# Pooled attention and a gated MLP on one core: first batch's left-over rows on ScalarE's queue, and a new order of work

## The chip, the core and the metric

The kernel runs on one core of a Trainium2 chip. The time is that of one execution on the device, in microseconds (us). Engines are named as in the profile: PE is TensorE, PEld its weight load, DVE is VectorE, ACT is ScalarE, POOL is GpSimd, SP is SyncE, which issues nearly all DMAs.

## The reference

Inputs: q, k, v of 8 batches x 8 heads x 576 rows x 64; weights w_in (512 x 1024), w_out (512 x 512) and w_sg (576 x 576), of which w_in and w_out arrive in 64-bit floats.

```
k_p = k.reshape(B, H, 72, 8, D).mean(axis=3);  v_p likewise
attn = softmax(q @ k_p.T / sqrt(D))                # 576 x 72 a head
x = (attn @ v_p), heads side by side               # 576 x 512 a batch
h = gelu(x @ w_in);  u, v = halves of h
v_n = (v - mean(v)) / sqrt(var(v) + 1e-6) * g_ln
gated = u * (w_sg @ v_n + b_sg)
out = x + gated @ w_out
```

## The kernel before

Batches go through the engines one after the other, each overlapped with its neighbours. A head pair is the unit of attention (four a batch, numbered 0 to 3). The work is cut into small generators, one for each letter, and a token such as `S0+1` advances step S for pair 0 of batch 1 by one piece. The table PROLOGUE (L23) lists all tokens of the program in the order in which they are issued; PERIOD is empty. Every engine works through its own instructions in that order and waits where an operand isn't there.

The letters, with what each does on the engines:
- A, B load half of k or v of a batch (tile kvraw, 512 KB), C a pair's q (tile qnat for batch 0, with pieces of 256 bytes; qraw later), E the left-over pooled rows of k and v that don't fill a tile (tile left, 256 KB in three DMAs). All of these, and the weights (lv, lu, lo, ls), go through `load`, with SP's queue by default.
- K pools k into kp and writes the scaled keys kbd (for batch 1 PE pools: `pool8`). K2 adds the left-over keys (lp). P pools v into vb.
- Q turns q into qT. S multiplies qT by kbd, takes the negated maximum (nmax, L559), the exponentials (e, L578, ten instructions on ACT) and the norm (L589, L590, L224).
- T and L turn the attention weights; V makes x from them; H and U make the two halves of gelu(x @ w_in); W the product with w_sg; O the product with w_out; Z and X store.
- v, u, o, s prepare the weights: each 64-bit weight is cut into a high and a low float (L286 to L294 and POOL's L231, L238).

Matmuls with the big weights run as three products of high and low parts. Rotating tiles: two `mps` and two `aps` PSUM tiles; a step that takes one waits until what used that tile two turns ago is read.

DMAs issued from SP and ACT carry one of eight completion semaphores in turn (DMAHW0 to DMAHW7); a DMA that comes round to a semaphore still in use waits for the earlier transfer to land, and what is behind it on that queue waits too.

The set OTHER (L87) names instructions that go to the second of two engines (for example `k01`: pooling of batch 0's second key half on DVE, otherwise POOL).

Of the kernel before, what the change touches and what calls it, by code (L numbers as in the profile page):

```python
# [28 lines left out]
u0 s2 S1+1 S1+1 s2 lu1 s2 H2+0 u1 C2+1 S0+1 Q2+1 S1+1 lo1 H2+0 S0+1 H0+0 o0 S1+1 P1+1 B0+1 u2 S2+1 o1 S0+1 H0+0 H2+0
H0+0 U0+0 S2+1 u3 V2+0 P1+1 S2+1 u2 u3 u2 U0+0 S1+1 H2+0 P0+1 S2+1 V1+0 u3 V3+0 P0+1 H0+0 H2+0 Q3+1 U1+0 P2+1 o2 H4+0  # L30
U1+0 H4+0 P2+1 S3+1 T0+1 S3+1 S3+1 H1+0 H2+0 H1+0 H0+0 S2+1 H4+0 H3+0 u3 A0+2 o2 H4+0 u2 P2+1 S3+1 H0+0 U2+0 S3+1 H3+0
L0+1 U3+0 A1+2 o2 H1+0 T0+1 P2+1 o2 H3+0 E0+2 T0+1 K2+2 C1+2 L0+1 Q1+2 L0+1 V0+1 V0+1 T1+1 T2+1 U2+0 H4+0 C0+2 H1+0
U3+0 K0+2 T1+1 T1+1 V1+1 Q0+2 K1+2 T2+1 T2+1 C3+2 T3+1 V1+1 H1+0 H3+0 B0+2 H3+0 H1+0 H3+0 B1+2 V2+1 H4+0 K2+2 H4+0
T3+1 H4+0 T3+1 P1+2 W2+0 V1+1 V3+1 V2+1 K2+2 P0+2 W2+0 C2+2 W1+0 V3+1 o3 K2+2 o3 V2+1 A0+3 S1+2 S1+2 S0+2 W0+0 W1+0 o3
S1+2 V0+1 o3 W1+0 S0+2 Q3+2 Q2+2 W0+0 S0+2 W3+0 W0+0 V0+1 W2+0 W3+0 V3+1 S1+2 S0+2 P2+2 S1+2 W1+0 H1+1 W2+0 V3+1 P2+2
C0+3 H3+1 H3+1 S3+2 H1+1 W0+0 A1+3 W3+0 S2+2 W3+0 S3+2 O0+0 H3+1 T0+2 H1+1 C1+3 K1+3 O0+0 O0+0 S0+2 S3+2 T0+2 T1+2
P2+2 O2+0 O2+0 U3+1 Z0+0 S2+2 H1+1 O2+0 P2+2 S2+2 H3+1 Z2+0 B1+3 H0+1 S3+2 U3+1 S3+2 H3+1 O1+0 H3+1 S2+2 Z0+0 H0+1
Z2+0 S2+2 L0+2 K0+3 V2+1 H1+1 O1+0 T2+2 V1+1 H4+1 L0+2 O1+0 H0+1 H4+1 H4+1 H0+1 T0+2 L0+2 H1+1 T0+2 H4+1 U0+1 L0+2
E0+3 H2+1 Z1+0 H0+1 V0+2 Q0+3 U0+1 O3+0 K2+3 H0+1 O3+0 L0+2 H2+1 H2+1 H4+1 Z1+0 B0+3 O3+0 P1+3 T1+2 U1+1 H2+1 K2+3
H2+1 T1+2 U2+1 H2+1 H4+1 T3+2 K2+3 T1+2 P0+3 Z3+0 A1+4 U1+1 H4+1 V0+2 H4+1 V1+2 K2+3 T2+2 W2+1 U2+1 S0+3 V1+2 W1+1  # L40
T2+2 W2+1 S0+3 T2+2 V1+2 W1+1 Q1+3 V2+2 K1+4 C2+3 W0+1 W2+1 T3+2 S0+3 Q2+3 C3+3 V2+2 T3+2 W1+1 W2+1 S0+3 T3+2 W3+1
T0+3 V3+2 Z3+0 S1+3 V0+2 W0+1 V3+2 W3+1 S1+3 S2+3 P2+3 W1+1 C0+4 V3+2 S2+3 T0+3 W0+1 V2+2 S1+3 S1+3 U2+2 H2+2 U2+2
S0+3 Q3+3 P2+3 P2+3 S3+3 C1+4 H2+2 W0+1 H2+2 O0+1 W3+1 W3+1 V1+2 O0+1 V3+2 A0+4 O1+1 P2+3 S3+3 S2+3 O0+1 V2+2 S2+3
# [903 lines left out]
```

## Time and profile before

| | |
|---|---|
| median of 3 runs (range) | 564.82 us (564.66 to 565.15) |
| the profiled execution | 566.29 us |
| its span, first to last instruction | 564.6 us |
| PE busy | 537.1 us, 95% |
| DVE, ACT, POOL busy | 421.1, 326.3, 287.2 us |
| DMA | 68.18 MB, mean 121 GB/s |

The profiled execution took 1.69 us more than its span and 1.47 us more than the median. All stretches below are in microseconds from the start of the span. A row of the timeline gives start, duration, engine, line, operation, tiles, and in brackets the idle time of that engine just before and what ended it.

### The profile page before, as it was taken

Reading aid. Unit: us, or ns where it says so; the run is one execution under the profiler, and the core shown is the slowest. Engines: PE = TensorE matmul, PEld = TensorE weight load, DVE = VectorE, ACT = ScalarE, POOL = GpSimd, SP = SyncE. Lnnn points to the kernel's source line nnn. Section 1 sums busy time; section 2 is a strip of 40 time slices with the busy share of each in tenths; the row PEclk is TensorE's granted clock in tenths of the full one; section 3 lists DMA queues with packets and bytes.
Section 4 is the critical chain, followed back from the end, with each engine's and each line's share of the span. In section 5 each row is a group of like instructions: output and inputs, shape, how many; then the busy total and the mean of one; then the engine's idle time right before and its main releaser. Section 6 shows DMA issues by size and latency. Waiting matters only on the chain.

```text
span 564.6 us, 10659 instructions
## 1 busy us (share of the span) xinstructions
PE 537.1 (95%) x3645; PEld 506.1 (90%) x3645; DVE 421.1 (75%) x655; ACT 326.3 (58%) x1057; POOL 287.2 (51%) x370
## 2 busy tenths in 40 slices
PE   4498898999999999999999999999999999999997
...
GB/s 211 299 307 157 113 135 48 130 59 161 132 176 102 91 157 129 138 102 139 128 135 96 127 111 149 158 146 103 120 152 86 128 65 73 69 24 1 22 43 106
DMA packets 186726, 68.18 MB, mean 121 GB/s; under 512 B 150832, under 2 KB 171056, under 8 KB 186672
## 3 DMA queue, kind: packets, MB, share of 16 engines
...
## 4 chain that ended last, share of the span: by engine, by line
PE 68%; DVE 9%; ACT 7%; SPq 7%; DMA 5%; issue 2%; POOL 1%; DVEq 0%; ACTq 0%; POOLq 0%
PE mps L141 56%; PE aps L141 12%; SPq L241 7%; ACT e L578 2%; DMA raw<-in_moe_w_out 1%; DVE nmax L559 1%; DMA qnat<-in_q 1%; DMA out<-y 1%; DVE e L224 1%; ACT L208 1%; DVE vbl L509 1%; DVE bst L746 1%; DVE vg L752 1%; DMA tfar<-y 1%; DMA y<-kfar 1%
## 5 line engine op out<-in xcount | busy, mean ns | idle before, releaser
L141 PE MATMUL mps<-xhl,wih 128*128 128x288 f32 x512 | 89.7, 297 | 1.4 <-ACT vg L742 1.0
L578 ACT ACTIVATE e<-aps,nmax 128x72 f32<-128x72 f32 x280 | 85.2, 355 | 9.7 <-DVE nmax L559 9.7
L141 PE MATMUL mps<-wih,xhl 128*128 128x512 f32 x256 | 83.8, 393 | 1.3 <-DVE wsl L321 1.3
L141 PEld LDWEIGHTS mps<-xhl,wih 128*128 128x128 f32 x512 | 75.4, 189 | 3.1 <-ACT vg L742 1.4
L578 ACT ACTIVATION_READ_ACCUMULATOR e<-aps,nmax 128x1 f32 x280 | 67.3, 241 | 0.0
L238 POOL TENSOR_TENSOR glo<-u,ghi 128x576 fp32r<-128x576 f32 x24 | 37.0, 1550 | 48.1 <-DVE ghi L213 24.4
L141 PEld LDWEIGHTS mps<-wih,xhl 128*128 128x128 f32 x256 | 48.1, 188 | 11.5 <-issue 1.7
L396 POOL TENSOR_TENSOR kvraw<-kvraw 128x512 f32<-128x512 f32 (+1 forms) x46 | 50.1, 1089 | 13.8 <-DMA kvraw<-in_k 7.6
L749 POOL TENSOR_TENSOR rstd<-mv,eps 128x1 f32<-128x1 f32 (+1 forms) x40 | 13.0, 325 | 86.5 <-DVE mv L747 83.9
L141 PE MATMUL mps<-wsh,vhh 128*128 128x288 f32 x256 | 55.1, 296 | 0.1
L141 PE MATMUL mps<-wsh,vhl 128*128 128x288 f32 x256 | 54.8, 295 | 0.0
L141 PE MATMUL mps<-xhl,wil 128*128 128x288 f32 x256 | 54.7, 295 | 0.0
L141 PE MATMUL mps<-wsl,vhh 128*128 128x288 f32 x256 | 54.7, 294 | 0.0
L141 PE MATMUL mps<-ghi,woh 128*128 128x288 f32 (+1 forms) x232 | 51.8, 302 | 0.1
L141 PE MATMUL mps<-glo,woh 128*128 128x288 f32 (+1 forms) x232 | 50.8, 298 | 0.4 <-POOL glo L238 0.4
L141 PE MATMUL mps<-ghi,wol 128*128 128x288 f32 (+1 forms) x232 | 50.7, 297 | 0.0
L141 PE MATMUL mps<-wil,xhl 128*128 128x512 f32 x128 | 50.0, 390 | 0.0
L798 DVE SCALAR_TENSOR_TENSOR mps<-mps,gcol,bbc 128x576 f32<-128x576 f32 x32 | 26.2, 820 | 30.8 <-PE mps L141 30.7
L659 ACT CAST ah<-al 128x640 fp32r<-128x640 f32 x24 | 17.6, 732 | 52.5 <-DMA al<-tfar 52.5
L141 PEld LDWEIGHTS mps<-wsh,vhh 128*128 128x128 f32 x256 | 41.2, 188 | 0.3 <-ACT u L784 0.3
L141 PEld LDWEIGHTS mps<-xhl,wil 128*128 128x128 f32 x256 | 41.2, 189 | 0.0
L141 PEld LDWEIGHTS mps<-wsh,vhl 128*128 128x128 f32 x256 | 41.0, 188 | 0.0
...
## 6 DMA issues: line engine op xcount, KB each, us to landing
...
```

The costliest lines, as they stand in the source:

```text
L141: nc.tensor.matmul(o, lhsT, rhs, start=start, stop=stop)
L208: nc.scalar.activation(early, eps[:, 0:1], func)
L224: (nc.gpsimd if key in OTHER else nc.vector).tensor_tensor(o, x, y, op=ALU.mult)
L238: (nc.vector if key in OTHER else nc.gpsimd).tensor_tensor(o, x, y, op=op)
L241: queue.dma_start(o, i)
L396: nc.gpsimd.tensor_tensor(t[:, :, 0:n * D], t[:, :, 0:n * D], t[:, :, n * D:2 * n * D], op=ALU.add)
L509: nc.vector.scalar_tensor_tensor(vbl[:, :, r], vp, head[:, h:h + 1], vbh[:, :, r].bitcast(F32), op0=ALU.mult, op1=ALU.subtract)
L559: nc.vector.tensor_reduce(out=nmax, in_=every.rearrange("p s (h k) -> p s h k", h=2), axis=AX.X, op=ALU.max, negate=True)
L578: nc.scalar.activation(e[:, i, h], slots[i][:, h], AF.Exp, bias=nmax[:, i, h:h + 1], **acc)
L659: nc.scalar.copy(ah, al)
L749: nc.gpsimd.tensor_tensor(rstd, mv[:, 1:2], eps[:n, 1:2], op=ALU.add)
L798: nc.vector.scalar_tensor_tensor(vs, vs, gcol[:, d:d + 1], bbc.rearrange("p (a n) -> p a n", a=2), op0=ALU.mult, op1=ALU.add)
```

## The change

Two edits. `load_left` issues its three DMAs on ACT's queue for batch 0 and on SP's for the others. PROLOGUE and OTHER are new tables: the same tokens in another order, and another choice of engines.

```
 PROLOGUE = """
-A0+0 C0+0 Q0+0 K0+0 E0+0 K2+0 lv0 K0+0 K0+0 K2+0 C1+0 K2+0 Q0+0 S0+0 Q1+0 v0 S0+0 S0+0 C2+0 A1+0 Q1+0 v0 v0 C3+0 Q2+0
+A0+0 C0+0 Q0+0 K0+0 E0+0 C1+0 K0+0 K2+0 lv0 C2+0 K2+0 K0+0 Q1+0 Q0+0 K2+0 S0+0 A1+0 v0 K1+0 S0+0 Q1+0 v0 S0+0 v0 Q2+0
...
 OTHER = """
-G02 G10 G20 G23 H02 H10 H11 H13 H21 P10 P11 Q00 Q01 T02 T11 V01 V03 V10 V21 V23 W01 W13 W23 X02 X03 X10 X20 X21 X22
-X23 Z0 c21 g12 g14 g20 g21 g22 h12 k00 k01 l0 n00 n23 o0d o0m o1m o2d o2m o3a p21 s2 u3a u3m v1m v3a x03 x12
+G00 G12 G13 G22 G23 H00 H02 H03 H11 H12 H13 H22 H23 K10 K11 Q00 Q01 T00 T13 V00 V02 V12 V13 V20 V23 W12 W13 X00 X01
+X02 X03 X11 X13 X20 X21 X23 Z0 c22 g02 g12 g13 g22 g24 h11 k00 l0 n23 o0m o1d o1m o2d o3d p21 s3 u0m u1m u2a u2m u3d
+u3m v2d v3d v3m x12
 """.split()
...
     def load_left(b):
         t = per.tile([P, 1, POOL * D], F32, name="left")
-        load(t[64:P, 0], keys(k[b])[:, P:2 * SP].rearrange("g r f -> r g f"))
+        queue = nc.scalar if b == 0 else nc.sync
+        load(t[64:P, 0], keys(k[b])[:, P:2 * SP].rearrange("g r f -> r g f"), queue)
         for gp in range(2):
-            load(t[32 * gp:32 * gp + 32, 0], keys(v[b])[2 * gp:2 * gp + 2, P:2 * SP].rearrange("g r f -> r g f"))
+            load(t[32 * gp:32 * gp + 32, 0], keys(v[b])[2 * gp:2 * gp + 2, P:2 * SP].rearrange("g r f -> r g f"), queue)
         st["left", b] = t
```

**Place 1: SP, from the first weight to w_out.** Before (raw is a weight as it arrives, kvraw a half of k, qnat and qraw are q, left the left-over rows of batch 1):

```order
L241 DMA raw<-in_moe_w_in 128x2x1024
L241 DMA qnat<-in_q 128x4x64 x2
L241 DMA qnat<-in_q 128x2x64
L241 DMA qnat<-in_q 128x4x64 x2
L241 DMA qnat<-in_q 128x2x64
L241 DMA kvraw<-in_k 128x2x512
L241 DMA qnat<-in_q 128x4x64 x2
L241 DMA qnat<-in_q 128x2x64
L241 DMA left<-in_k 64x1x512
L241 DMA left<-in_v 32x1x512 x2
L241 DMA qraw<-in_q 32x18x32 x4
L241 DMA raw<-in_moe_w_out 128x4x512
```

Now:

```order
L242 DMA qnat<-in_q 128x4x64 x2
L242 DMA qnat<-in_q 128x2x64
L242 DMA raw<-in_moe_w_in 128x2x1024
L242 DMA qnat<-in_q 128x4x64 x2
L242 DMA qnat<-in_q 128x2x64
L242 DMA kvraw<-in_k 128x2x512
L242 DMA qnat<-in_q 128x4x64 x2
L242 DMA qnat<-in_q 128x2x64
L242 DMA kvraw<-in_k 128x2x512
L242 DMA raw<-in_moe_w_out 128x4x512
```

Three DMAs of q (pair 1) stand ahead of the first weight; batch 1's left and qraw no longer stand ahead of w_out (they are issued behind the second part of w_in), and the first half of batch 1's k does. By the semaphores in turn, the first weight now waits for one of the two v parts of batch 0's left to land, and w_out for the first DMA of pair 2's q, which is issued right behind the first weight.

**Place 2: ACT, its first instructions.** Before:

```order
L406 ACT_TABLE_LOAD
L406 ACTIVATE kbd<-mps 64x2x72
L471 ACTIVATE kbd<-mps 64x4x16
L286 ACTIVATE mps<-raw 128x512
L578 ACTIVATE e,ssum<-mps,nmax 128x72 x10
```

Now:

```order
L242 DMA left<-in_k 64x1x512
L242 DMA left<-in_v 32x1x512 x2
L408 ACT_TABLE_LOAD
L408 ACTIVATE kbd<-mps 64x2x72
L473 ACTIVATE kbd<-mps 64x4x16
L287 ACTIVATE mps<-raw 128x512
L580 ACTIVATE e,ssum<-mps,nmax 128x72 x10
```

Batch 0's left is issued by ACT ahead of its table load (from SP it stood behind qnat of pair 0, ahead of the first weight). What follows is the same.

**Place 3: ACT, from the exponentials of batch 0's pair 1 (e_246 before, e_230 now).** raw_231 and raw_265 are w_out, qT_237 and qT_258 the queries of pair 3. Before:

```order
L578 ACTIVATE e_246,ssum_247<-mps_222,nmax_235 128x72 x10
L286 ACTIVATE top_266<-raw_231 128x512
L215 COPY qT_237<-aps_238 128x576
L294 CAST wih_101<-top_210 128x512
L215 COPY ah_296<-aps_271 128x576
L286 ACTIVATE top_298<-raw_231 128x512
L578 ACTIVATE e_316,ssum_317<-mps_277,nmax_283 128x72 x10
L215 COPY kp_302<-aps_303 128x128
L578 ACTIVATE e_363,ssum_364<-mps_285,nmax_312 128x72 x10
```

Now:

```order
L580 ACTIVATE e_230,ssum_231<-mps_218,nmax_224 128x72 x10
L287 ACTIVATE top_269<-raw_265 128x512
L216 COPY qT_258<-aps_259 128x576
L287 ACTIVATE top_288<-raw_265 128x512
L580 ACTIVATE e_290,ssum_291<-mps_271,nmax_284 128x72 x10
L580 ACTIVATE e_309,ssum_310<-mps_278,nmax_307 128x72 x10
L236 ACTIVATE raw_145<-raw_145 128x512
L295 CAST wih_101<-top_215 128x512
L499 ACTIVATE vb_117<-aps_341,head_82 128x4x64 x2
```

The cut of w_out and the copy of pair 3's queries still stand behind those exponentials; the copies of the weight wih, of ah and of kp that stood around the next exponentials are later or on DVE (kp, ah).

## Rows read from the trace of the kernel before

**Rows 1.** The page: busy time of PE, and PE's busy tenths in 40 slices of the span.
```profile
PE 537.1 (95%) x3645; PEld 506.1 (90%) x3645; DVE 421.1 (75%) x655; ACT 326.3 (58%) x1057; POOL 287.2 (51%) x370
...
PE   4498898999999999999999999999999999999997
```
**Rows 2.** Busy time by stretch: busy us (and instructions) of PE, PEld, DVE, ACT, POOL, then the granted clock of TensorE, the DMA engines' busy share and GB/s.
```profile
0.00:30.00 30.00, 14.54 (x76) 12.29 (x77) 19.61 (x27) 15.77 (x67) 12.14 (x30) 0.95 0.91 265
30.00:60.00 30.00, 27.08 (x176) 22.87 (x176) 26.96 (x39) 27.28 (x96) 20.38 (x20) 0.99 0.68 194
60.00:100.00 40.00, 36.65 (x249) 33.48 (x248) 35.96 (x63) 33.37 (x96) 31.38 (x39) 1.00 0.38 109
100.00:540.00 440.00, 437.24 (x3013) 416.99 (x3012) 325.08 (x511) 249.06 (x802) 219.07 (x280) 1.00 0.47 110
540.00:564.60 24.60, 21.55 (x139) 20.45 (x137) 13.51 (x22) 0.80 (x2) 4.24 (x3) 1.00 0.41 73
```
**Rows 3.** Timeline of SP, DMAs as issued: start, duration (several DMAs of a kind together).
```profile
0.80 0.45 SPq L241 DMA_DIRECT2D kvraw<-in_k  x1
...
2.91 0.68 SPq L241 DMA_DIRECT2D left<-in_k  x1
3.63 1.23 SPq L241 DMA_DIRECT2D left<-in_v  x2
4.90 0.58 SPq L241 DMA_DIRECT2D raw<-in_moe_w_in  x1
...
12.06 0.47 SPq L241 DMA_DIRECT2D kvraw<-in_k  x1
...
14.27 0.57 SPq L241 DMA_DIRECT2D left<-in_k  x1
14.88 1.23 SPq L241 DMA_DIRECT2D left<-in_v  x2
16.16 2.29 SPq L241 DMA_DIRECT2D qraw<-in_q  x4
18.49 0.65 SPq L241 DMA_DIRECT2D raw<-in_moe_w_out  x1
```
**Rows 4.** Timeline of the first 13 us, the chain to the first scores.
```profile
4.33 1.89 DVE L399 TENSOR_REDUCE kp<-kvraw 128x128 f32<-128x1024 f32 x1 [1.80 <-DMA kvraw<-in_k]
...
7.45 1.28 ACT L406 ACT_TABLE_LOAD   x1 [7.45 <-PE mps L428]
7.57 1.01 DVE L399 TENSOR_REDUCE lp<-left 128x64 f32<-128x512 f32 x1 [1.35 <-DMA left<-in_v]
...
9.34 0.76 DVE L213 COPY qT<-aps 128x576 f32<-128x576 f32 x1
...
10.25 2.74 PE L141 MATMUL mps<-kbd,qT 128*128 128x144 f32 x10 [1.07 <-DVE qT L213]
```
**Rows 5.** Timeline from 12 to 29 us: first weight, exponentials, scores of pairs 2 and 3, and what they waited for.
```profile
12.17 0.63 ACT L286 ACTIVATE mps<-raw 128x512 f32<-128x512 f32 x1 [2.74 <-DMA raw<-in_moe_w_in]
...
13.97 0.32 ACT L578 ACTIVATE e<-mps,nmax 128x72 f32<-128x72 f32 x1 [1.17 <-DVE nmax L559]
...
21.88 1.49 PE L141 MATMUL mps<-kbd,qT 128*128 128x144 f32 x10 [0.50 <-DVE top L289]
...
23.84 0.90 DVE L224 TENSOR_TENSOR e<-e,mps 128x720 f32<-128x720 f32 x1
...
25.33 0.66 ACT L286 ACTIVATE top<-raw 128x512 f32<-128x512 f32 x1 [2.00 <-DMA raw<-in_moe_w_out]
25.89 0.63 ACT L215 COPY qT<-aps 128x576 f32<-128x576 f32 x1
...
26.57 2.48 PE L141 MATMUL mps<-kbd,qT 128*128 128x144 f32 x10 [3.20 <-ACT qT L215]
```
**Rows 6.** Busy time by stretch as in rows 2, for the start.
```profile
26.50:30.00 3.50, 3.43 (x16) 3.43 (x17) 3.36 (x4) 3.50 (x17) 1.27 (x1) 0.56 1.06 418
2.00:8.00 6.00, 1.73 (x7) 1.27 (x7) 2.52 (x3) 0.55 (x1) 2.82 (x9) 1.00 0.98 263
...
12.00:14.00 2.00, 1.83 (x10) 1.30 (x8) 0.98 (x2) 0.66 (x2) 0.00 (x0) 1.00 0.56 126
14.00:18.00 4.00, 2.20 (x15) 1.81 (x15) 3.44 (x7) 4.00 (x22) 0.29 (x1) 1.00 1.02 255
18.00:20.00 2.00, 0.51 (x5) 0.54 (x6) 2.00 (x2) 1.33 (x4) 2.00 (x2) 1.00 1.07 138
...
26.00:36.00 10.00, 9.43 (x68) 9.43 (x69) 8.91 (x14) 9.38 (x48) 3.10 (x4) 0.83 1.06 391
```
**Rows 7.** Timeline of ACT at 31 us: the copy of batch 1's first pooled keys out of PSUM.
```profile
31.54 0.27 ACT L215 COPY kp<-aps 128x128 f32<-128x128 f32 x1 [0.35 <-PE aps L141]
```
**Rows 8.** Timeline of PE: pooling of k and v, and one matmul of H of batch 0 with its wait.
```profile
29.70 7.16 PE L141 MATMUL aps<-kvraw,ident 128*128 128x128 f32 x60
...
59.64 0.47 PE L141 MATMUL mps<-wih,xhl 128*128 128x512 f32 x1 [1.32 <-DVE wsl L321]
```
**Rows 9.** Waits in total: engine, line, waited for; us, times, longest.
```profile
PE aps L180 <- ACT x L215: 1.2, 2, 0.7
PE aps L180 <- DVE al L648: 1.2, 1, 1.2
...
PE mps L141 <- ACT vg L742: 1.0, 1, 1.0
```

More of the change, by code (lines that the diff above doesn't have):

```diff
@@ L29 @@
[L29 to L43, printed above, removed]
@@ new lines @@
+H1+1 O2+0 T0+2 O0+0 O1+0 S2+2 O1+0 B1+3 Q0+3 Z0+0 P2+2 O2+0 S3+2 H3+1 O1+0 P2+2 Z2+0 H1+1 U3+1 S2+2 V1+1 H3+1 Z0+0
+S3+2 H2+1 H1+1 K0+3 T0+2 U3+1 Z2+0 S2+2 T2+2 S3+2 E0+3 H4+1 S3+2 H2+1 L0+2 H4+1 H4+1 H0+1 H3+1 H0+1 U2+1 H2+1 K2+3
+H4+1 L0+2 O3+0 H2+1 H0+1 T0+2 H4+1 C2+3 L0+2 B0+3 L0+2 V0+2 H4+1 T1+2 O3+0 H0+1 U2+1 T1+2 H0+1 O3+0 K2+3 H0+1 C1+3
+L0+2 P1+3 K2+3 H2+1 T1+2 U0+1 H4+1 U1+1 Z1+0 H4+1 Q1+3 H2+1 U0+1 U1+1 V1+2 T2+2 K2+3 Z3+0 V0+2 W2+1 S0+3 V1+2 Z1+0
+V1+2 W2+1 W3+1 T2+2 T2+2 T3+2 Z3+0 P0+3 V2+2 S0+3 W0+1 S0+3 W3+1 V0+2 S0+3 W0+1 T3+2 S0+3 W1+1 T3+2 T0+3 T3+2 V2+2
@@ new lines @@
+W0+1 Q2+3 C0+4 A0+4 V3+2 S1+3 W1+1 V3+2 S1+3 V3+2 S1+3 V2+2 C3+3 H2+2 U2+2 W3+1 W0+1 S1+3 Q3+3 S2+3 P2+3 V1+2 S3+3
+W2+1 W3+1 H2+2 W2+1 S2+3 W1+1 S3+3 U2+2 W1+1 S3+3 T1+3 Q0+4 O0+1 V3+2 P2+3 O0+1 O0+1 H2+2 V2+2 O1+1 T0+3 S1+3 O1+1
+O2+1 S2+3 P2+3 H2+2 O1+1 V0+2 S3+3 Z1+1 K0+4 A1+4 S2+3 O2+1 O2+1 H1+2 H4+2 S2+3 H2+2 H1+2 S3+3 H1+2 H3+2 H4+2 H2+2
+H4+2 K1+4 Z1+1 L0+3 H4+2 Z2+1 T0+3 O3+1 O3+1 H3+2 P2+3 H1+2 H1+2 H3+2 H4+2 O3+1 H0+2 H4+2 U3+2 Z2+1 L0+3 H3+2 H1+2
+H0+2 B0+4 L0+3 H4+2 T0+3 L0+3 V0+3 L0+3 U1+2 Z0+1 H4+2 E0+4 U3+2 T1+3 U0+2 H0+2 Z0+1 T2+3 C1+4 H3+2 T1+3 H0+2 H0+2
@@ new lines @@
+T1+3 T3+3 H3+2 V1+3 U1+2 K2+4 H0+2 P0+4 U0+2 T2+3 A0+5 K2+4 Z3+1 T2+3 K0+5 T2+3 W0+2 B1+4 W0+2 V0+3 P1+4 W2+2 V2+3
+Q1+4 K2+4 V1+3 V1+3 W0+2 K2+4 V0+3 T3+3 Z3+1 T3+3 V0+3 W1+2 W0+2 W2+2 V2+3 W1+2 T3+3 C2+4 W3+2 V3+3 W1+2 W3+2 V3+3
+W1+2 W3+2 W3+2 W2+2 C3+4 S0+4 W2+2 S0+4 A1+5 S0+4 S1+4 V2+3 S1+4 V3+3 Q3+4 V2+3 O0+2 Q2+4 O0+2 S0+4 T0+4 S1+4 H1+3
+S2+4 O0+2 P2+4 V1+3 S2+4 S1+4 H1+3 K1+5 P2+4 O1+2 H1+3 Z0+2 O1+2 S0+4 S3+4 T0+4 Z0+2 H1+3 O1+2 O2+2 O2+2 S3+4 T1+4
+S1+4 S2+4 H0+3 O2+2 S3+4 C1+5 H2+3 S2+4 Z2+2 H1+3 B1+5 H0+3 H2+3 V3+3 S3+4 S3+4 P2+4 Z2+2 S2+4 T0+4 L0+4 U3+3 Q1+5
```

82 lines of the change are left out of this document (41 added, 41 removed).

## The prediction

> **What bounds the kernel now.** I read the page's busy line first: PE is busy 537.1 of 564.6 us, so reordering can win at most the 27.5 us in which PE stands, and nothing that leaves PE's work as it is can win more [rows 1]. The 40 slices say where it stands: the digits are low in the first two slices, a little low to the seventh, and 9 from there to the last [rows 1]. The table of stretches puts numbers on that: PE stands 30.0 - 14.5 = 15.5 us before 30 us, 2.9 us from 30 to 60, 3.4 us from 60 to 100, only 2.8 us in the 440 us up to 540, and 3.1 us at the end [rows 2]. So the long middle has nothing to give, and the start decides. In the stretches 30 to 60 and 60 to 100 DVE and ACT are busy about nine tenths too (27.0 and 27.3 of 30, then 36.0 and 33.4 of 40): there PE waits for them here and there, and work moved between them matters [rows 2].
>
> Next the start itself. The timeline of SP shows every DMA going out in line: left at 2.91 and 3.63, the first weight at 4.90, w_out only at 18.49 [rows 3]. The DMA engines are full almost all the time, but at 138 GB/s while qraw with its small pieces is under way, 255 and 263 GB/s with q and left among the rest, and 391 GB/s with big pieces only; from 12 to 14 us they are half idle, because SP was held up behind full semaphores [rows 6]. ACT then stands 2.00 us for w_out until 25.33; the queries of pair 3 are copied behind that, at 25.89, and PE, which stood 3.20 us for them, starts pair 3's scores at 26.57 [rows 5]. Two things follow: all pooling comes after those scores on PE, and the scores run at half clock. The granted clock is 0.56 from 26.5 to 30 us, that is mostly the 1.2 GHz level, and the same ten matmuls took 2.48 us against 1.49 us at 21.88 [rows 5, 6].
>
> **The change part by part.**
>
> (a) Batch 0's left goes out on ACT's queue. ACT does nothing before its table load at 7.45 [rows 4], and three issues cost 0.68 + 1.23 us by SP's rows [rows 3], so they are free there: the cover is 7 us of idle ACT. On SP 1.9 us of issue time goes away. The direct gain is near nothing: DVE did wait 1.35 us for left, but its lp ends at 8.58 and the first scores at 10.25 come by another chain, from kp over PE, the table load until 8.73, ACT's and DVE's kbd and the copy of qT [rows 4]. That chain begins when the first kvraw lands at 4.33 [rows 4], and here the edit may cost: left's 256 KB now share the DMA engines with kvraw from the first moment, where they stood behind it. All of it ahead of kvraw is 256 KB at 263 GB/s, 1.0 us; none is 0. I take +0.5 us on the first scores, since the two queues start together. On this the Trainium skill (DMA: Bandwidth & Descriptors, section "Issuing engines are not separate DMA queues") speaks against the edit: DMAs of different issuers run on the same 16 engines and interleave, and only the time to issue them is saved. By that rule alone the edit gives no gain, which agrees with the chain in rows 4.
>
> (b) The first weight goes out behind pair 1's q. Those 320 KB at 263 GB/s are 1.2 us at most [rows 6]; nothing is lost if the engines are as full as before. Before, the weight landed for ACT at 12.17, and the exponentials behind it on ACT then stood 1.17 us for nmax until 13.97 [rows 5]. So a delay of 1.2 us just fits. I take 0; over that it is the rival below.
>
> (c) w_out is issued earlier. Ahead of it on SP left (0.57 + 1.23 us) and qraw (2.29 us) of batch 1 are gone, and a half of k (0.47 us) is new [rows 3]. In bytes: qraw's 288 KB at 138 GB/s are 2.1 us, left's 256 KB at 255 GB/s 1.0 us, and the 512 KB of k at 391 GB/s cost 1.3 us; the half-idle stretch from 12 to 14 us gives up to 0.9 us back [rows 6]. The sum is w_out some 1.8 to 2.7 us sooner, at about 23 us, when ACT comes free (25.33 - 2.00 = 23.33) [rows 5]. So ACT's wait of 2.00 us goes. What is late next is the PSUM tile for pair 3's scores: it is free when DVE's norm of pair 1 is done, at 24.74 before [rows 5]. With some 0.2 us left over from (a) I put those scores at 25.0 instead of 26.57: -1.6 us, between -2.0 and -0.9.
>
> (d) PE's gap ahead of them falls from 3.20 to about 1.2 us, so the clock should stay up: the ten matmuls give 2.48 - 1.49 = 1.0 us back [rows 5]. Ends: 0, if the clock falls all the same, and -1.1 with the first matmuls of the pooling. I take -1.0 us.
>
> (e) The copy of batch 1's first pooled keys goes from ACT, where it took 0.27 us at 31.54 [rows 7], to DVE, behind a maximum, w_out's three steps and a norm. The last pooling on PE needs that PSUM tile. PE pools 60 matmuls in 7.16 us [rows 8], so it reaches that point after three quarters of 64, some 5.8 us after its start at about 26.3, hence at 32; DVE is free at 33 to 34 by its rows for the same work. That is +0.8 us, between 0 and +1.7.
>
> (f) Batch 0's H stood 1.32 us for DVE's wsl at 59.64 [rows 8]. In the new order wsl and the low part of x follow each other with one maximum between. I take half, -0.6 us (0 to -1.3).
>
> (g) Batches 2 to 7 have another order too, but the stretch has only 2.8 us of idle PE in 440 us [rows 2], and the tail ends with the same matmuls, additions and stores. Its cover is the next batch's matmuls; I put it at 0, and the turning of batch 1 (1.2 and 1.0 us of waits for DVE and ACT [rows 9]) at 0 as well, between -1 and +1.5 us together.
>
> The sum: -1.6 - 1.0 + 0.8 - 0.6 = -2.4 us. The profiled execution took 566.29 us, 1.69 us over its span; it would become 563.9 us. It stood 1.47 us over the median of the runs, so the median goes from 564.82 to 562.4 us.
>
> **The rivals.** *Given back before 100 us.* The start gains as above, but DVE, with the copies and norm it took over, is nine tenths busy from 30 to 100 us [rows 2], and PE then waits longer for it at kp, at the turning and at wsl. With (e) at +1.7, (f) at 0 and 0.7 more at the turning, -2.6 + 2.4 gives 564.6 us, no change. For it speaks rows 9, where all three waits are of this kind; against it that ACT is relieved.
>
> *The first weight is late.* The mechanism ends slower. In ACT's order the weight's first step stands ahead of all exponentials. It is issued behind pair 1's q, and the next half of k, issued at 12.06 before [rows 3], now goes out some 4 us sooner and shares the engines with it. If its landing slips by more than the 1.17 us of slack, everything behind moves: 1.2 us by q and up to 512 KB at 263 GB/s = 1.9 us by k are 3.1 us, less 1.2 us of slack, 1.9 us. Then pair 1's exponentials end at 25.2, pair 3's scores stay at 26.6 or later, the gap and the half clock stay, (e) still costs 0.8 and the first half of k up to 0.5 more: 566.1 us. It decides at a landing past 13.3 us. For it speaks that the engines are full from 2 us on; against it that the bytes ahead of the weight grow by 320 KB only.
>
> *Left takes its full share.* If all of left lands ahead of kvraw, the first scores come 1.0 us later instead of 0.5 (256 KB at 263 GB/s [rows 6]) and the rest of the sum stands: -2.4 + 0.5 = -1.9 us, 562.9 us. That is inside the forecast's range, and I give it 0.15 of the forecast's chance. This is what the Trainium skill's sentence on interleaving, cited in (a), would come to here.
>
> **How the numbers follow.** A measurement of this kernel tells 0.2%, 1.1 us, from no change. The forecast (a net gain of more than that, 560.4 to 563.7 us) gets 0.60: the wait for w_out is on the chain, and its bytes leave that chain. Given back before 100 us: 0.24. Late weight and other waits that the new order makes: 0.16. The range of 8 in 10 goes from 560.6, near the sum of the good ends (-2.0 - 1.1 - 1.3 = -4.4), up to 566.0 us, which takes in the case without change and leaves out about half of the slow one.
>
> **What would show it.** In the changed profile: ACT not idle for w_out, pair 3's scores at about 25 us with a granted clock of 1.0 from 26 to 30, the pooling over by 35 us (36.9 before), batch 0's first H about 2 us sooner, and PE's idle time before 60 us at about 16 us against 18.4 before. I am wrong if ACT's first exponentials start after 14.5 us, if PE's idle time from 60 to 540 grows by more than 1 us, or if the median is 564 us or more.

## The result, and the profile after

The changed kernel takes 568.1 us (median of 19 runs, 564.9 to 569.5) against 564.7 us: the ratio is 1.0054, 95% interval [1.0042, 1.0066]. A second set on another occasion gave 567.4 against 564.5, ratio 1.0039 [1.0025, 1.0054]. The forecast was 562.4, and a gain; it is a loss of 2.9 to 3.4 us, outside the range given. Single runs far outside all others are left out of every median (here one of 668.6 us with the change and one of 1075.2 without it, in e9 two of 1876).

The profiled execution took 566.71 us with a span of 564.9, so it is one of the better ones of the changed kernel, 1.4 us under its median. The profiled execution of the kernel before was the other way about, 1.47 us over its median: the two traces lie 0.4 us apart, the medians 3.4. That matters below: what a typical execution loses on top isn't in this trace.

Busy time by stretch, columns as in [rows 2]:

```profile
0.00:30.00 30.00, 16.98 (x97) 15.00 (x98) 18.66 (x29) 16.24 (x77) 11.12 (x30) 1.00 0.99 289
30.00:60.00 30.00, 26.83 (x166) 22.46 (x165) 28.23 (x43) 26.96 (x93) 20.22 (x21) 1.00 0.71 193
60.00:100.00 40.00, 37.24 (x261) 34.60 (x262) 37.77 (x63) 31.75 (x85) 29.03 (x36) 1.00 0.37 104
100.00:540.00 440.00, 435.05 (x2998) 415.28 (x2997) 327.77 (x504) 255.40 (x814) 207.86 (x271) 1.00 0.47 109
540.00:564.90 24.90, 20.61 (x132) 19.51 (x130) 13.62 (x21) 1.25 (x2) 5.67 (x4) 1.00 0.41 72
```

Subtract PE's busy time from each stretch. Before 60 us PE stands 16.2 us; before the change it stood 18.4 [rows 2]. The start has 2.2 us less of it. But from 100 to 540 it stands 4.95 us and not 2.76, and at the end 4.3 and not 3.05: the gain is given back there, and the span is where it was.

Timeline of the start (start, duration, engine, line, operation, in brackets the idle time before and what ended it), to hold against [rows 4, 5]:

```profile
0.80 0.66 ACTq L242 DMA_DIRECT2D left<-in_k  x1
1.49 1.30 ACTq L242 DMA_DIRECT2D left<-in_v  x2
...
6.90 1.08 PE L538 MATMUL aps<-ident,qnat 128*128 128x128 f32 x4 [6.90 <-DMA qnat<-in_q]
8.71 1.28 ACT L408 ACT_TABLE_LOAD   x1 [8.71 <-PE mps L430]
11.51 2.74 PE L142 MATMUL mps<-kbd,qT 128*128 128x144 f32 x10 [1.59 <-DVE qT L214]
11.82 0.63 ACT L287 ACTIVATE mps<-raw 128x512 f32<-128x512 f32 x1 [1.28 <-DMA raw<-in_moe_w_in]
15.23 0.32 ACT L580 ACTIVATE e<-mps,nmax 128x72 f32<-128x72 f32 x1 [2.79 <-DVE nmax L561]
...
23.82 0.71 ACT L287 ACTIVATE top<-raw 128x512 f32<-128x512 f32 x1
24.38 0.68 ACT L216 COPY qT<-aps 128x576 f32<-128x576 f32 x1
25.70 1.46 PE L142 MATMUL mps<-kbd,qT 128*128 128x144 f32 x10 [1.72 <-ACT top L287]
27.00 7.36 PE L142 MATMUL aps<-kvraw,ident 128*128 128x128 f32 x64
```

PE waits for q until 6.90 and the first scores start at 11.51, 1.26 us later than before. ACT no longer waits for w_out (no bracket at 23.82), pair 3's scores start at 25.70 and run at full clock (1.46 us). So far the forecast's mechanism. The pooling behind them, 64 matmuls from 27.00, waits for nothing. What follows wasn't forecast: the wait for wsl (the low part of w_sg) stands ahead of H2 (the first block of batch 0's x @ w_in) now and is longer than the old one [rows 8].

```profile
50.53 1.59 POOL L239 TENSOR_TENSOR xhl<-x,xhl 128x576 fp32r<-128x576 f32 x1 [2.06 <-ACT x L216]
50.89 1.79 DVE L291 SCALAR_TENSOR_TENSOR raw<-top 128x512 int32<-128x512 int32 x1
52.59 0.90 DVE L561 TENSOR_REDUCE nmax<-aps 128x10 f32<-128x720 f32 x1
53.41 0.74 DVE L322 TENSOR_TENSOR wsl<-mps,wsh 128x576 fp32r<-128x576 f32 x1
54.21 0.50 PE L142 MATMUL mps<-wih,xhl 128*128 128x512 f32 x1 [2.21 <-DVE wsl L322]
...
110.16 2.69 PE L142 MATMUL aps<-kbd,qT 128*128 128x144 f32 x20 [0.87 <-DVE qT L544]
124.69 1.46 PE L142 MATMUL aps<-kbd,qT 128*128 128x144 f32 x10 [1.43 <-DVE e L225]
```

DVE's write at 50.89 takes 1.79 us where the same operation takes 0.69 elsewhere; the two rows at 110 and 124 us are batch 2's scores, which did not wait at all before. The end, of the changed kernel:

```profile
559.11 2.11 SPq L242 DMA_DIRECT2D out<-yend  x2
561.32 0.42 SPq L242 DMA_DIRECT2D out<-yrow  x1
...
560.65 0.42 DVE L861 TENSOR_TENSOR yrow<-aps,xrow 128x256 f32<-128x256 f32 x1 [1.01 <-PE aps L142]
```

and of the kernel before:

```profile
560.05 0.84 SPq L241 DMA_DIRECT2D out<-yend  x2
560.99 0.45 SPq L241 DMA_DIRECT2D out<-yrow  x1
...
561.59 0.42 DVE L859 TENSOR_TENSOR yrow<-aps,xrow 128x256 f32<-128x256 f32 x1 [1.01 <-PE aps L141]
```

The last addition is over at 561.07 now and at 562.01 before, but the span ends 3.8 us after it and not 2.6.

### The profile page after: what moved, and what is told of

Its sections match the earlier page's. It is cut to its first block, busy times and chain, and to the rows that moved or that the text cites. A ratio compares the mean times of both kernels' runs of the same rounds, so it can differ in the third digit from the quotient of the medians.

```text
span 564.9 us, 10669 instructions
## 1 busy us (share of the span) xinstructions
PE 536.7 (95%) x3645; PEld 506.8 (90%) x3645; DVE 426.0 (75%) x657; ACT 331.6 (59%) x1067; POOL 273.9 (48%) x362
## 4 chain that ended last, share of the span: by engine, by line
PE 62%; DVE 16%; ACT 7%; DMA 6%; SPq 4%; issue 3%; POOL 2%; DVEq 0%; ACTq 0%; POOLq 0%
PE mps L142 52%; PE aps L142 9%; ACT e L580 4%; SPq L242 4%; DMA al<-tfar 2%; DMA qraw<-in_q 1%; DVE qT L544 1%; DVE nmax L561 1%; DVE bst L748 1%; DVE raw L291 1%; DVE raw L230 1%; DMA qnat<-in_q 1%; DVE vg L754 1%; DMA kvraw<-in_v 1%; DVE top L290 1%
## 5 line engine op out<-in xcount | busy, mean ns | idle before, releaser
L239 POOL TENSOR_TENSOR glo<-u,ghi 128x576 fp32r<-128x576 f32 x30 | 44.0, 1475 | 68.8 <-ACT ghi L216 37.7
L398 POOL TENSOR_TENSOR kvraw<-kvraw 128x512 f32<-128x512 f32 (+1 forms) x48 | 52.6, 1097 | 28.9 <-DMA kvraw<-in_k 16.6
L580 ACT ACTIVATION_READ_ACCUMULATOR e<-aps,nmax 128x1 f32 x280 | 65.4, 234 | 0.0
L751 POOL TENSOR_TENSOR rstd<-mv,eps 128x1 f32<-128x1 f32 (+1 forms) x40 | 11.5, 288 | 75.2 <-DVE mv L749 75.1
L754 DVE SCALAR_TENSOR_TENSOR vg<-vg,mv,rstd 128x512 f32<-128x512 f32 (+1 forms) x40 | 38.9, 982 | 7.6 <-POOL rstd L752 7.3
L664 DVE TENSOR_TENSOR al<-al,ah 128x640 fp32r<-128x640 f32 x24 | 23.7, 986 | 23.7 <-ACT ah L661 23.6
```

Source lines behind the costliest of these rows:

```text
L239: (nc.vector if key in OTHER else nc.gpsimd).tensor_tensor(o, x, y, op=op)
L398: nc.gpsimd.tensor_tensor(t[:, :, 0:n * D], t[:, :, 0:n * D], t[:, :, n * D:2 * n * D], op=ALU.add)
L580: nc.scalar.activation(e[:, i, h], slots[i][:, h], AF.Exp, bias=nmax[:, i, h:h + 1], **acc)
L664: nc.vector.tensor_tensor(lo, al, ah.bitcast(F32), op=ALU.subtract)
L751: nc.gpsimd.tensor_tensor(rstd, mv[:, 1:2], eps[:n, 1:2], op=ALU.add)
L754: nc.vector.scalar_tensor_tensor(vg, vg, mv[:, 0:1], rstd.broadcast_to([n, DF2]), op0=ALU.subtract, op1=ALU.mult)
```

## The experiments

Each was run in turn with the kernel before on the same chip, whose median was 564.4 to 564.6 us each time. "The changed kernel" below is 567.6 us, the median of its 30 runs. Most edits only move tokens of the table; they are shown with their neighbours. In the names, v0, v1, u0 and u1 are blocks of w_in, wil its low part, al the low part of the turned attention weights, and el the tail columns of the exponentials.

### The same again, and left back on SP's queue

e1_again is the changed kernel unaltered. e2_left_on_sp has one line back:

```
-        queue = nc.scalar if b == 0 else nc.sync
+        queue = nc.sync
```

> The changed kernel once more, to see how far its runs lie apart and to have a second profile. Both theories: a median of 567 to 569 us, runs from 565 to 569.5. If the second profile is of a run near 568.5 us, the theory of the rest expects over 6.5 us of idle PE between 100 and 540 us (4.95 in the first profile, 2.76 before); the theory of the start expects the surplus before 100 us.

> The changed kernel with batch 0's left issued by SP again, the new order kept. Theory of the start (left on ACT's queue delays the first q and k, and that delay stays): the first scores return from 11.5 us to 10.0 to 10.5 us, and the time falls by 1 to 3 us to 565 to 567 us. Theory of the rest (the start is not where the time is lost): within 1 us of the changed kernel, 567 to 569 us.

Measured: 567.4 us (1.0039 [1.0025, 1.0054]) and 566.5 us (1.0038 [1.0024, 1.0051]). The loss is real. In e2 the first scores are back at 10.30 us, inside the 10.0 to 10.5 expected, but the time falls by 0.9 to 1.1 us only, so left's queue is about a third of the loss (566.5 lies within what the theory of the start said and within 1 us of e1, so it doesn't part the two theories). The new trace of the same kernel is as instructive as the first, since it is 1.0 us longer. Its PE stands 4.3 us from 100 to 540 us, no more than the 4.95 of the first, so the difference lies ahead of that:

```profile
22.58 1.30 POOL L239 TENSOR_TENSOR wil<-raw,top 128x512 fp32r<-128x512 f32 x1
22.72 1.71 DVE L291 SCALAR_TENSOR_TENSOR raw<-top 128x512 int32<-128x512 int32 x1
...
26.53 1.46 PE L142 MATMUL mps<-kbd,qT 128*128 128x144 f32 x10 [0.85 <-DVE e L225]
55.01 0.50 PE L142 MATMUL mps<-wih,xhl 128*128 128x512 f32 x1 [2.17 <-DVE wsl L322]
93.13 0.40 PE L142 MATMUL aps<-ah,vbh 128*128 128x288 f32 x1 [1.17 <-DVE al L650]
```

The first trace has the same two operations the other way round:

```profile
22.47 1.85 POOL L239 TENSOR_TENSOR wil<-raw,top 128x512 fp32r<-128x512 f32 x1
22.47 0.69 DVE L291 SCALAR_TENSOR_TENSOR raw<-top 128x512 int32<-128x512 int32 x1
...
90.81 0.40 PE L142 MATMUL aps<-ah,vbh 128*128 128x288 f32 x1 [1.17 <-DVE al L650]
```

Two things differ. At 22.5 us one of DVE and POOL is held up by the other, and whichever starts first is not; when DVE loses, pair 3's scores start at 26.5 and not 25.7. And from H2 to the wait for al it takes 93.13 - 55.01 = 38.1 us here, 90.81 - 54.21 = 36.6 there, with the same work: the granted clock from 50 to 60 us was 0.83 here, behind the 2.2 us in which PE stood, and 1.00 there, behind the same wait.

The traces of the runs below bear out both. With left on ACT's queue, first scores of 2.74 us and the wait for wsl as it was, H2 starts at 54.1 to 54.5 us if DVE's write isn't held up (the first trace, e6, e9, e17) and at 55.0 to 56.1 if it is (e1, e7, e8, e15); e14 delays DVE by other means. From H2 to the wait for al it takes 36.6 to 36.8 us where the granted clock from 50 to 60 us is 1.00 (the first trace, e6, e7, e8, e14, e17), and 38.0 to 38.2 where it is 0.83 (e1, e2, e9, e15, e16). Which of the two comes first at 22.5 us goes with the ten scores of pair 1 just before: they took 2.41 to 2.63 us where DVE did (the first trace, e6, e17) and 2.69 to 2.77 where POOL did (e1, e5, e7, e8).

### Halves of the new order

e3_new_start takes the new order and choices up to batch 0's first H and the old ones behind it, e4_new_rest the other way round.

> The new order and the new choice of engines for batches 0 and 1 and the weights up to the first H of batch 0, left on ACT's queue, then the old order and old choice. Theory of the start: slow like the changed kernel, 567 to 569 us. Theory of the rest: the forecast gain of the start shows alone, 562.5 to 564.3 us, with the pooling starting near 27 us.

> The other half: the old order up to the first H of batch 0, left on SP's queue, then the new order with the new choice of engines for batches 2 to 7. Theory of the start: 564 to 565.5 us, as before. Theory of the rest: 567 to 569.5 us, with runs that lie 3 us or more apart, and more idle PE between 100 and 540 us than before (2.76 us).

Measured: 576.3 us (1.0210 [1.0189, 1.0232]) and 575.2 us (1.0183 [1.0163, 1.0204]), both far from what either theory said, and 7.6 us and more above either whole order. From 60 to 200 us PE stood 7.9 and 11.7 us, against 5.1 with the new order whole and 3.8 with the old. The cut itself makes waits, so the two say nothing about the halves; a list of tokens can't be parted in the middle of a batch.

### The wait ahead of H2: removed, or filled

e5_wsl_early puts s0's copy and subtraction ahead of DVE's work on u1, pair 2's low part ahead of the maximum, and U0 ahead of U1:

```
-u1 u0 V2+0 V3+0 u1 s2 s0 C3+1 S0+1 S0+1 s0 V3+0 lu1 s2 V2+0
+u1 u0 V2+0 V3+0 s0 s0 u1 s2 C3+1 S0+1 V2+0 S0+1 V3+0 lu1 s2
```

e6_fill leaves the wait and gives PE something to do in it:

```
+        if b == 0 and i == 2:
+            for _ in range(16):
+                nc.tensor.transpose(st["fill"][:, 6 * P:7 * P], swap, ident)
         o = mtile()[:, 0]
```

> The changed kernel, with the low half of w_sg's first block (s0, its ACT copy and its DVE subtraction) and pair 2's low half moved ahead of the DVE chain of w_in's u1 block, and columns U0 multiplied before U1 in batch 0. Theory A (what was lost is the 2.2 us wait for wsl ahead of H2, and the half clock that follows it in most runs): the wait shrinks to under 0.7 us, H0 starts 1.5 us or more sooner, the granted clock over 50-60 us is 1.00, and the median falls from 567.4-568.2 to 563.5-565.5 us. Theory B (any lead is eaten by 130 us, since batch 2's scores wait for ScalarE's exponentials and VectorE's normalisation and not for TensorE): H0 starts sooner just the same, but the waits near 110 and 124 us (0.87 and 1.43) grow by about what was gained, and the median falls by what the clock cost alone, to 566-567 us.

> The changed kernel with 16 transposes of constants (about 1.9 us of TensorE work by 0.118 us each) put into the 2.2 us in which TensorE waits for wsl ahead of H2; they write to an unused part of a PSUM buffer and nobody waits for them. H2 starts when it did. If the half clock behind that wait is what slows most runs, the granted clock over 50-60 us is 1.00 in this profile, the stretch from H2's start to the wait for al near 91-93 us takes 36.6 and not 38.1 us, and the median falls by 1 to 2 us, to 565.5-566.7 us, with less spread. If the clock falls for another reason, or its cost is hidden later, the median stays at 567.2-568.4 us.

Measured: 568.0 us (1.0057 [1.0041, 1.0072]) and 566.2 us (1.0023 [1.0009, 1.0038]). In e5, which came out as neither theory said, the wait went and came back: PE then stood 1.22 us at 61.45 and 1.15 us at 64.62 for batch 1's norm on DVE, which the moved work had delayed. DVE has no slack there, so putting one thing first only renames the wait. Four of e5's six runs had a mean granted clock of 0.999 or 1.000 and took 566.2 to 568.2 us all the same: the clock is not the whole of it. In e6 H2 starts when it did (54.12), and only the clock differs. Busy time from 50 to 60 us, columns as in [rows 2], of e1_again:

```profile
50.00:60.00 10.00, 7.83 (x38) 6.50 (x37) 9.86 (x14) 8.55 (x45) 5.88 (x6) 0.83 0.32 81
```

and e6_fill:

```profile
50.00:60.00 10.00, 9.56 (x59) 8.16 (x58) 9.86 (x14) 8.53 (x45) 6.41 (x6) 1.00 0.33 82
```

Over whole runs the mean granted clock was 1.000 in 9 of e6's 12 runs and in 1 of the changed kernel's 30. That agrees with the clock's part in the loss, some 1.4 us (567.6 - 566.2), and so do the changed kernel's own runs: four have 0.999 or 1.000 and take 564.6 to 566.7 us, the 26 others (0.986 to 0.997) have a median of 567.8. The times of e6 with the clock at 1.000 still went from 564.0 to 567.8, so it isn't the whole spread.

### The end and batch 2

e7_tail takes the order of the last product's O, X and Z from the kernel before. e8_mid makes two moves on DVE in batch 2:

```
-V2+1 K2+2 o3 C3+2 Q0+2 o3
+Q0+2 V2+1 K2+2 o3 C3+2 o3
...
-Q3+2 A0+3 S1+2
+A0+3 S1+2 Q3+2
```

> The changed kernel with the order of the last product's pieces (O, X, Z of batch 7) taken from the kernel before, all else as changed. Theory: the changed order ends 3.6-3.8 us after the last addition where the old one ended after 2.6, since xrow's copy stands between the additions and the eight store issues of two blocks reach both queues at once, so that the first half row's store is issued 1.7 us after it is ready. With the old order the span ends 2.4-2.8 us after the last addition and the median falls by 0.8 to 1.2 us to about 566.4-567. Rival: the end depends on how many stores are in flight and not on this order: no change, 567.2-568.2 us.

> The changed kernel with two moves on VectorE in batch 2: pair 0's q transposed ahead of w_out's last block and pair 1's x copy, and pair 3's q transposed behind the normalisation of pair 1 instead of ahead of it. If the waits of TensorE at 110 us (0.87) and 124.7 us (1.43) are where the lead of the start was given back, they shrink to under 0.3 and under 0.9 us and the median falls by 1.2 to 1.6 us, to 566-566.8. If the lead is eaten anyway (the time lost turns up in a wait further on), the median stays at 567.2-568.2 us.

Measured: 566.05 us (1.0027 [1.0011, 1.0043]) and 565.9 us (1.0019 [1.0005, 1.0033]). In e7 the first half row goes out as soon as it is ready (added until 559.96, issued at 560.38), and the span ends 564.3 - 561.40 = 2.9 us after the last addition (2.4 to 2.8 was expected):

```profile
560.38 0.45 SPq L239 DMA_DIRECT2D out<-yrow  x1
...
560.98 0.42 DVE L858 TENSOR_TENSOR yrow<-aps,xrow 128x256 f32<-128x256 f32 x1 [1.01 <-PE aps L139]
```

In e8 the wait at 110 us is gone and the other halved, and neither came back further on (PE stands 2.3 us from 100 to 540):

```profile
125.13 1.46 PE L139 MATMUL aps<-kbd,qT 128*128 128x144 f32 x10 [0.68 <-ACT vg L741]
```

### DVE and POOL out of each other's way, and everything together

e9_port moves one token, pair 0's el on POOL, behind the split of v0. e10_v03 gives pair 3's low part (POOL's 1.59 us at 50.53) to DVE. e11_all has both and the edits of e7 and e8; e12_all_sp is e11 with left on SP's queue.

```
-S0+0 S3+0 S3+0 B0+0 o0 K0+1 S2+0 v0 P1+0
+S3+0 S3+0 B0+0 o0 K0+1 S2+0 v0 S0+0 P1+0
...
-V00 V02 V12 V13
+V00 V02 V03 V12 V13
```

> The changed kernel with one move on GpSimd: pair 0's tail copy el stands behind the split of w_in's v0 block instead of ahead of it, so that GpSimd's subtraction for wil is over before 22.4 us, when VectorE writes the high words of the next block. Theory C: in seven traces of this order the two operations start within 0.15 us of each other; where GpSimd is first VectorE's takes 1.70 to 1.77 us, where VectorE is first 0.69, and after 1.7 pair 3's scores start at 26.5 instead of 25.7 us and the following 50 us come 0.8 to 2 us later. With the move VectorE's operation takes 0.69 in every run, pair 3's scores start by 25.7, and the median falls by 0.8 to 1.5 us to 566-567 with a smaller spread. Rival: that 1 us is absorbed in the waits up to 60 us in any case, and the median stays at 567.2-568.2.

> The changed kernel with one key moved: the low half of pair 3 of batch 0 is subtracted by VectorE and no longer by GpSimd (its 1.59 us at 50.53). Theory: GpSimd's operation lengthens VectorE's write of the u1 block's high words from 0.69 to 1.79 us at 50.9, which stands ahead of the wsl that H2 waits for. The write takes 0.69 us, the wait ahead of H2 shrinks from 2.2 to 1.0-1.3 us, H2 starts about 1 us sooner, and the median falls by 0.8 to 2 us (the upper end if the clock then stays up over 50-60 us). Rival: the lead is eaten at batch 1's and batch 2's scores, and the median stays at 567.2-568.2.

> The changed kernel with four repairs together: el behind the v0 split on GpSimd, pair 3's low half on VectorE, the two moves of VectorE in batch 2, and the old order of the last product. If the places named so far are where the time went, the repairs add up to most of what they gave one by one (1.3 to 2 us each for the middle and the end, about 1 us each for the start): 562.5 to 564.5 us, below the kernel before. If they overlap (one lead, given back in whichever wait comes next), the median stays at 565-566.5.

> The same four repairs with the first batch's left-over rows on SP's queue as before. In the unrepaired order that queue was worth 0.9 us (567.4 against 566.5). If the left-over rows' place is a cost of its own (first scores 1.2 us later), this is 0.5 to 1.2 us below the run with four repairs; if the start is hidden behind later waits, the two are within 0.4 us.

Measured: 566.0 us (1.0020 [1.0006, 1.0034]), 565.2 us (1.0007 [0.9996, 1.0017]), 562.4 us (0.9968 [0.9951, 0.9986]) and 563.6 us (0.9978 [0.9962, 0.9994]). e9's trace is of its longest run (568.1): POOL's subtraction was over at 22.59, DVE's write took 0.75 us, and pair 3's scores followed pair 2's without a wait, but the clock fell behind H2. The smaller spread that was expected of e9 did not come (564.2 to 568.1). In e10 the write ahead of wsl takes its 0.69 us and the wait for wsl is halved. The rows of e9, then of e10:

```profile
21.30 1.29 POOL L236 TENSOR_TENSOR wil<-raw,top 128x512 fp32r<-128x512 f32 x1
22.59 0.75 DVE L288 SCALAR_TENSOR_TENSOR raw<-top 128x512 int32<-128x512 int32 x1
```

```profile
50.42 0.69 DVE L288 SCALAR_TENSOR_TENSOR raw<-top 128x512 int32<-128x512 int32 x1
...
52.65 0.50 PE L139 MATMUL mps<-wih,xhl 128*128 128x512 f32 x1 [1.08 <-DVE wsl L319]
```

One by one the repairs of e7 to e10 give 1.5, 1.7, 1.6 and 2.4 us, 7.2 in all; together 5.2. Singly, e6 to e9 stand at the edge of what these runs can tell from the changed kernel; together there is no doubt, and e11 beats the kernel before by 0.32% [0.14%, 0.49%]. Its stretches:

```profile
0.00:30.00 30.00, 18.52 (x108) 16.86 (x109) 19.87 (x32) 17.39 (x84) 10.87 (x30) 0.83 0.97 284
30.00:60.00 30.00, 27.38 (x170) 22.94 (x169) 28.26 (x45) 27.71 (x88) 20.21 (x21) 1.00 0.74 202
...
100.00:540.00 440.00, 437.64 (x3017) 417.82 (x3016) 328.07 (x507) 256.47 (x816) 206.72 (x271) 1.00 0.47 108
```

PE stands 14.1 us before 60 us and 2.4 us from 100 to 540, where the changed kernel has 16.2 and 4.95. One thing in the traces of e10, e11 and e16 comes from no edit: their first ten scores took 1.46 us and not 2.74, so that the work up to 25 us came about 1.1 us sooner, and from 15 to 20 us the granted clock was 0.50. Of e11:

```profile
11.67 1.46 PE L139 MATMUL mps<-kbd,qT 128*128 128x144 f32 x10 [1.62 <-DVE qT L211]
```

e11's column below has that 1.1 us in it, and some of PE's busy time is slow matmuls. e12's trace is without it: there H2 starts at 51.78 us and PE stands 14.5 us before 60. The same points of the program in four traces (us; the old order has other work between them, so its column compares only roughly):

| | before | changed | again | e11 |
|---|---|---|---|---|
| pair 3's scores, batch 0 | 26.57 | 25.70 | 26.53 | 24.55 |
| H2, batch 0 | 55.30 | 54.21 | 55.01 | 52.02 |
| first W, batch 0 | 99.78 | 96.69 | 99.00 | 95.13 |
| first O, batch 0 | 126.18 | 125.90 | 128.16 | 122.80 |
| last addition over | 562.01 | 561.07 | 562.33 | 556.84 |
| end of the span | 564.6 | 564.9 | 565.9 | 559.7 |

### Left alone, and the other outcome forced

e13_left_alone is the kernel before with `load_left` as changed. The other four force the outcome of the race at 22.5 us, or take the means of forcing it apart. e14 puts two copies of 72 columns from SBUF ahead of DVE's work on v1, e15 one from PSUM, both into a new small tile; e16 makes the copy in place in PSUM; e17 has the tile and no copy.

```
+    pad = const.tile([P, 72], F32, name="pad")                     # e14, e15, e17
...
+            if name == "v" and c == 1:
+                nc.vector.tensor_copy(pad, bits[:, 0, 0:72].bitcast(F32))           # e15
+                nc.vector.tensor_copy(bits[:, 0, 0:72], bits[:, 0, 0:72])           # e16
```

> The kernel before with one part of the change alone: the first batch's left-over rows on ScalarE's queue, order and keys as before. The two pairs of runs on this point disagree: on the unrepaired new order the left-over rows were better on SP's queue by 0.9 us, on the repaired one better on ScalarE's by 1.2. If the part has a price of its own (the transfer takes its share while q's first block loads: the first transposes at 6.9 and not 5.6 us, the first scores 1.2 us later), this is 0.5 to 1.2 us above the kernel before, 565.1 to 565.8. If the later start is hidden behind the weights' chain, it is within 0.4 us of it.

> The changed kernel with two small copies of constants (128x72) on VectorE ahead of its first operation on w_in's v1 block, which put its write of the high words (22.5 to 22.7 us) some 0.2 to 0.4 us later and so behind the start of GpSimd's subtraction for wil in every run. Theory C (whichever of the two starts first decides, and it is a race in the changed kernel): the write takes 1.6 to 1.8 us in the profile, pair 3's scores start at 26.5 us or later, and the median is 0.5 us or more above the changed kernel's 567.4 to 568.2, and 1.5 to 3 us above the run in which GpSimd's subtraction comes early (566.1). Rival (the long write is not what costs): 567.2 to 568.2, as the changed kernel.

> The changed kernel with one copy of 72 columns from PSUM on VectorE ahead of the shift of w_in's v1 block: a delay of some 0.15 to 0.25 us and not 2.6 as the two copies from SBUF, so that GpSimd's subtraction for wil (22.5 us) starts first and VectorE's write of the high words behind it. Theory C: the write takes 1.6 to 1.8 us in the profile, pair 3's scores start at 26.4 to 26.9 us, and the median is 567.8 to 569.5, that is 1.5 us or more above the run with GpSimd out of the way (566.1) and a little above the changed kernel, in which either comes first. Rival (which of them is first does not matter for the end): 567.2 to 568.2 or less.

> The changed kernel with the small copy of 72 columns on VectorE made in place in PSUM, with no new tile: the same delay of about 0.25 us as in the run before, which stood at 570.4. Theory C: VectorE's write starts behind GpSimd's, takes 1.3 to 1.8 us, pair 3's scores start at 26.4 to 26.9 us, and the median is 567.8 to 569. If it is 570 again, the order of the two operations is worth 2 us or more; if it is 567.5 or less, what slowed the run before was the tile that it added.

> The changed kernel with the small tile alone (72 columns in SBUF, one of them set once by GpSimd at the start) and no added copy. It moves the addresses of the tiles behind it and nothing else. If addresses don't matter: 567.2 to 568.3 us, as the changed kernel. If the tile is what slowed the two runs that held it: 569 us or more.

Measured: e13 565.85 us (1.0021 [1.0010, 1.0031]): in the old order the left-over rows on ACT's queue cost 1.2 us by themselves. Its first scores wait for q as the changed kernel's do:

```profile
6.96 1.08 PE L535 MATMUL aps<-ident,qnat 128*128 128x128 f32 x4 [6.96 <-DMA qnat<-in_q]
11.56 2.74 PE L139 MATMUL mps<-kbd,qT 128*128 128x144 f32 x10 [2.67 <-DVE qT L211]
```

In the new order the two pairs (e1 and e2, e11 and e12) point opposite ways by 0.9 and 1.2 us with intervals that overlap, so there its price stays open. A part of the second may be the fast first scores: five of e11's ten runs have the mean clock of its profiled one (0.990 to 0.991) and a median of 561.9 us, the five others 563.9, and none of e12's (563.6) has it.

e14 took 572.0 us (1.0145 [1.0120, 1.0171]) and missed its aim: the two small copies were held until POOL was done and delayed DVE by 2.5 us.

```profile
21.22 2.54 DVE L292 COPY pad<-ident 128x72 f32<-128x72 f32 x2
...
22.40 1.30 POOL L240 TENSOR_TENSOR wil<-raw,top 128x512 fp32r<-128x512 f32 x1
```

e15 delayed it by 0.27 us and made the write start behind POOL's operation, but took 570.4 us (1.0119 [1.0100, 1.0139]), more than expected. e16 and e17 tell why: 568.4 us (1.0072 [1.0059, 1.0085]) with the delay and no tile, 570.7 us (1.0118 [1.0094, 1.0142]) with the tile and no delay. The tile costs some 3 us on its own (below). The clean run is e16. Its median is within what the theory said and 2.4 us above e9, in which POOL is out of the way; the 0.8 us to the changed kernel, in which either comes first, are not clear of the spread. Its trace misses one point: pair 3's scores start at 25.33, not at 26.4 or later, since this is one of the executions with fast first scores:

```profile
21.39 1.30 POOL L239 TENSOR_TENSOR wil<-raw,top 128x512 fp32r<-128x512 f32 x1
...
21.81 1.42 DVE L293 SCALAR_TENSOR_TENSOR raw<-top 128x512 int32<-128x512 int32 x1
...
25.33 1.46 PE L142 MATMUL mps<-kbd,qT 128*128 128x144 f32 x10 [0.57 <-DVE e L225]
```

## Why the prediction was wrong, step by step

**What bounds the kernel** was read right as to where PE stands, and wrong in the conclusion that the middle "has nothing to give" and so nothing to lose. 2.8 idle us in 440 is what the old order made of it; a new order isn't bound to it.

**(a) Left on ACT's queue, +0.5 (0 to +1.0).** Mis-sized: the first scores came 1.26 us later, and alone it costs 1.2 us (e13). The chain was the wrong one. The first half of k landed at 4.43 as against 4.33 [rows 4]; it is q, behind k, that came late (first transposes 6.90, 5.63 before), and q was not in the sum.

**(b) The first weight, 0.** Right: ACT had it at 11.82, before at 12.17 [rows 5]. The first exponentials did start after 14.5 (15.23), but for the scores and not for the weight; that rival didn't happen.

**(c) w_out sooner, -1.6 (-2.0 to -0.9).** The mechanism was right: ACT's wait is gone. The size was half: in the first trace the scores start at 25.70, 0.87 us sooner, since the later first scores of (a) move what stands ahead of them; with left back on SP's queue (e2) they start at 24.66. When POOL wins at 22.5 us, nothing is left of it: 26.46 to 26.54 in e1, e5, e7 and e8.

**(d) The clock stays up, -1.0.** In the first trace it does, and the scores take 1.46 us, at the 2.4 GHz level. Going by the mean clock, 26 of the 30 executions don't keep it: in e5, e7 and e8 the granted clock from 26 to 30 us is 0.58, 0.58 and 0.73, on the way to the 1.2 GHz level, and in e1 it falls behind H2 instead. Nor did the old kernel have 1.0 us to give back: 24 of its 118 runs beside the experiments had a mean granted clock of 0.999 or 1.000 and a median of 564.4 us, the 94 others 564.5. So, again by the mean clock, the half clock of the old trace cost the end next to nothing, and the sum's second largest term was not there to be won.

**(e) The copy of kp, +0.8 (0 to +1.7).** It cost nothing: PE pools the 64 matmuls from 27.00 in 7.36 us without a wait; a wait of 0.54 us for POOL's el comes behind them. PE's idle time before 60 us is 16.2 us, where "about 16" was said, but that is luck: (c) gave half, (e) took nothing, and (f) went the wrong way.

**(f) The wait for wsl, -0.6 (0 to -1.3).** This step failed in sign. The wait is 2.0 to 2.2 us in every trace in which the new order stood unedited there, where the old one was 1.32. "One maximum between" was read off the order, but not what stands ahead of it on DVE: the work on u1, whose last write is stretched from 0.69 to 1.79 us by POOL's subtraction (e10 shows both). And a longer wait isn't only its own length: in five of the ten traces that have it (e1, e2, e9, e15, e16) the clock falls behind it, 38.1 us for work of 36.6 (e1), and e6, which keeps PE busy there, has the clock up in 9 of 12 runs.

**(g) The rest, 0 (-1 to +1.5).** This step failed too, and is the largest. Two waits at batch 2's first scores (0.87 and 1.43 us, e8), and 1.0 to 1.2 us more between the last addition and the end, from stores that keep SP's queue (e7). In the first trace a lead of 3.1 us at the first W of batch 0 is 0.3 us at its first O, since batch 2's queries and norms stand behind other work on DVE: PE stands 2.3 us from 100 to 126, and not at all in the old trace.

**The rivals.** "Given back before 100 us" had the right idea and the wrong place: at 100 us the lead was there, and it was lost from 100 to 126 us, at the end, and to a lower clock. All three signs of being wrong came: exponentials at 15.23 us, 1.6 us more of idle PE from 60 to 540, and the median. The forecast worked from one trace of the old kernel, 1.47 us over its median; the first trace of the changed kernel is one of its good ones, and the runs' spread of 4.6 us (1.9 before) shows how much the new order leaves to chance. "Left takes its full share" came near in size (1.26 us for 1.0), by q and not by k.

What stays open: the spread that is left with the clock at 1.000 (e6), and left's price in the new order.
